# An eighth slot in the ring of loaded weight pieces, with the first tokens' mask in bf16 and two gate tiles moved to the first tokens' pool

## The chip, the cores and the metric

One Trainium2 chip, and of it one core. The metric is the device time of one execution in microseconds (us), lower is better; the time of a kernel is the median of its runs. In this text PE is TensorE, PEld its weight load, DVE is VectorE, ACT is ScalarE, POOL is GpSimd and SP is SyncE, from whose queue every DMA of this kernel is issued.

## The reference: attention with a memory, then a squared-ReLU feed-forward layer

There are 4 batches, 8 heads, 576 positions and 64 channels a head. Causal softmax attention is mixed with a linear memory read by a gate for each head; the result, 2304 tokens of 512 channels, goes through a layer of 2048 hidden units.

```python
scores = where(causal, -1e9, q @ k.T / 8)
a = exp(scores - scores.max(-1)); a /= a.sum(-1) + 1e-9
phi = lambda x: where(x > 0, x, exp(x) - 1) + 1
mem = (phi(q) @ M_prev) / (phi(q) @ z_prev + 1e-6)
g = 1 / (1 + exp(-beta))                      # for each head
x = g * mem + (1 - g) * (a @ v)               # 2304 x 512
h = x @ w_in                                  # 512 x 2048
out = maximum(h, 0) ** 2 @ w_out              # 2048 x 512
```

## The kernel before

**Weights.** They come in as 64-bit floats, seen as pairs of 32-bit words, in 32 pieces of 128 x 512 values (512 KB each): four groups of w_in pieces and four of w_out in turn, four pieces to a group. `load_weight` (L269 to 272) issues the load of a piece into the ring "raw" of `NRAW` slots, 4 KB per partition each. `to_float` (L191 to 205) makes 32-bit floats: a shift on DVE (L199) or its counterpart on ACT (L197), a rescale on ACT (L200) and a merge on DVE (L202) that writes the ring "fc" (12 slots) and is the last reader of the raw slot. After each fourth piece `weight_scale` (L221) takes products of the four pieces on PE (L228) and a root on DVE, and `halves` (L242) splits each piece into two fp16 parts, one on ACT (L246) and one on DVE (L247). `pieces` (L281) walks over the pieces; before piece n it asks for loads until `min(32, n + NRAW)` are out, so the load of piece n + NRAW - 1 is written in the program just ahead of the conversion of piece n. The first four loads are asked for inside the first tokens' load sequence `SEQ`.

**First tokens.** The first 64 positions of all batches and heads go first, in two groups (`first_tokens`, L308): scores (L339), phi (L344 to 346), the softmax with `mask0` added to the scores from PSUM (L351 to 359), the memory read with `gib` and the softmax's scale with `g1b` (L358, L371), outputs (L385 to 392), squares and a root for a scale (L397 to 403), two fp16 parts (L406, L407), and a DMA transpose into xT (L410). They have high priority. `gates` (L143) makes the gate tiles from beta.

**Then** the units of attention, one for a batch, a pair of heads and some query tiles (L453), merged with the rest of the weights and with the feed-forward layer of the first tokens, `moe(0)` (L922), whose first matmul (L973) needs both xT transposes and the first group of w_in. The blocks of 256 tokens that follow need the transposes of L724, which stand behind unit 3's results and two splits on DVE (L723).

**What sets the order.** Each engine, and SP's queue too, runs its instructions in the order in which the tile framework wrote them down; that order comes from priorities (the order of the program, the first tokens ahead) and estimated times when the kernel is compiled. Orders are also forced by hand: ACT and DVE work on pieces from 8 on, and PE's first attention work, stand behind the first tokens' operations (`gate`, `later`, `put`), and work on pieces from 16 on behind the split of piece 11.

**Memory.** `cp` holds constants for the whole kernel. The pool `rw` holds the rings raw and fc; `tp`, opened inside it, holds what the first tokens need and is closed before the pieces are converted further; the second pool of split weights, `wpl2`, is laid over its place, and the pool `late` with attention buffers of later units is laid over the place of `rw`. In both a tile waits for the former tiles under it.

```python
def pieces(n0, n1):
    for n in range(n0, n1):
        while len(loaded) < min(NU, n + NRAW):
            ahead()
        to_float(n)
```

Of the kernel before, what the change touches and what calls it, by code (L numbers as in the profile page):

```python
# [8 lines left out]
F32 = mybir.dt.float32  # L9
F32R = mybir.dt.float32r  # L10
F16 = mybir.dt.float16
BF16 = mybir.dt.bfloat16
# [6 lines left out]
B, H, S, D = 4, 8, 576, 64  # L19
# [3 lines left out]
P = 128  # L23
# [22 lines left out]
PHI = 1  # L46
ZW = D + 1
MW = 576
NRAW = 7
NFC = 12  # L50
NR0 = 16
TINY = 2.0**-80
# [17 lines left out]
GN = GB * NP  # L70
# [28 lines left out]
def fused_kernel(ctx: ExitStack, tc: tile.TileContext, t0_d, kk_d, qv_d, beta, w_in, w_out, out):  # L99
# [3 lines left out]
    cp = ctx.enter_context(tc.tile_pool(name="cp", bufs=1))  # L103
# [30 lines left out]
    def load_beta():  # L134
        nc.sync.dma_start(gpm, beta)
        gates()

    gi = cp.tile([P, H], F32, name="gi")
    gs = cp.tile([P, H], F32, name="gs")
    gib = cp.tile([P, GN], F32, name="gib")  # L140
    g1b = cp.tile([P, GN], F32, name="g1b")

    def gates():  # L143
        nc.scalar.activation(gpm, gpm, AF.Exp, scale=-1.0)
        nc.vector.tensor_scalar(out=gpm, in0=gpm, scalar1=1.0, scalar2=None, op0=ALU.add)
        for b in range(GB):
            nc.vector.tensor_copy(gib[:, b * NP : (b + 1) * NP], gp)
        nc.vector.reciprocal(gpm, gpm)
        nc.vector.reciprocal(gi, gm)
        nc.vector.tensor_scalar(out=gm, in0=gm, scalar1=-1.0, scalar2=1.0, op0=ALU.mult, op1=ALU.add)  # L150
        nc.vector.reciprocal(gm, gm)
        nc.vector.tensor_scalar(out=gs, in0=gm, scalar1=SC, scalar2=None, op0=ALU.mult)
        for b in range(GB):
            nc.vector.tensor_scalar(
                out=g1b[:, b * NP : (b + 1) * NP], in0=gp, scalar1=-1.0, scalar2=1.0, op0=ALU.mult, op1=ALU.add
            )
        nc.vector.reciprocal(g1b, g1b)

    mask0 = cp.tile([P, D], F32, name="mask0")
    nc.vector.tensor_copy(mask0[:D], mask[:D, 448 : 448 + D])  # L160
    nc.vector.tensor_copy(mask0[D:], mask[D:, 512 : 512 + D])

# [103 lines left out]
    def ring(tag, shape, dtype, bufs):  # L266
        return more[-1].tile(shape, dtype, tag=tag, name=tag, bufs=bufs)

    def load_weight(n):  # L269
        raw[n] = ring("raw", [P, 1024], U32, NRAW)  # L270
        w, r0, cs = wsrc[n]
        nc.sync.dma_start(raw[n], w[r0 : r0 + P, cs])
# [3 lines left out]
    def ahead():  # L276
        if len(loaded) < NU:
            load_weight(len(loaded))
            loaded.append(1)
# [5 lines that stand above are left out]
# [11 lines left out]
    def weights():  # L296
        with tc.tile_pool(name="rw", bufs=1, side="right") as rw:
            more.append(rw)
            with tc.tile_pool(name="tp", bufs=1, reuse_waits="tile") as tp:
                first_tokens(tp, ahead)  # L300
            yield
            yield from pieces(0, NR0)
            wpl.append(ctx.enter_context(tc.tile_pool(name="wpl2", bufs=1, reuse_waits="tile")))
            yield from pieces(NR0, NU)
        more.append(ltx.enter_context(tc.tile_pool(name="late", bufs=1, reuse_waits="tile")))
        yield

    def first_tokens(tp, ahead):  # L308
# [2 lines left out]
        ng = B // GB  # L311
        bc = [P, GN, D]
        tr, sp, et, ft, st = ({} for _ in range(5))

        for g in range(ng):
            tr[g] = tp.tile([P, TW], F32, name=f"tr{g}")
# [825 lines left out]
```

## Time and profile before

| what | value |
|---|---|
| median of 3 runs | 560.11 us (559.65 to 561.05) |
| the profiled execution | 561.7 us, of which its span is 559.9 us |
| mean granted PE clock | 0.976 of full speed |
| PE busy | 522.5 us, 93% |
| DVE busy | 451.9 us, 81% |
| ACT busy | 412.0 us, 74% |
| DMA queue of the loads | 70.57 MB, 53.7% of 16 engines' span |
| load of one weight piece | 512 KB, 6.6 us (w_in) and 7.5 us (w_out) from issue to landing, medians |

Times inside the profile count from the start of the span. A share over the whole span mixes stages: the loads and the conversion of the weights lie in the first 110 us, the rest is attention and the feed-forward layer.

### The profile page before, as it was taken

The numbers are of one execution on the slowest core, as the hardware profiler recorded it, in microseconds if no ns is written. First come the engines' busy times: TensorE is split into PE (matmuls) and PEld (weight loads), VectorE is DVE, ScalarE is ACT, GpSimd is POOL, SyncE is SP. The second block draws the span as 40 slices with busy tenths as digits, with TensorE's granted clock in tenths as the row PEclk, the third lists the DMA queues.
The fourth block names the chain that finished last, engine by engine and source line by source line (L and its number), as shares of the span: only waits on it lengthen the run. The fifth ranks groups of instructions, "written<-read, shape, count | busy, mean of one in ns | idle before, by whom it ended". The sixth has DMA issues, their size and how long they took to land.

```text
span 559.9 us, 12611 instructions
## 1 busy us (share of the span) xinstructions
PE 522.5 (93%) x4767; PEld 369.5 (66%) x4767; DVE 451.9 (81%) x1421; ACT 412.0 (74%) x884; POOL 17.8 (3%) x20
## 2 busy tenths in 40 slices
PE   5655999998999999999989999999999999999996
PEld 4544766656777767667756777667766866447766
DVE  6898879998997999999967778888686788745645
ACT  3699997894788879989867777889666734566252
POOL 1000030111010000000000000000000000000000
PEclk9967999998999999999989999999999999999999
DMA  8968931497576759988746476481755320100002
GB/s 309 405 215 247 325 109 39 124 160 186 117 157 152 174 136 158 179 171 183 131 90 150 115 138 123 76 145 47 115 94 80 91 39 1 39 1 1 1 1 75
DMA packets 133132, 71.37 MB, mean 127 GB/s; under 512 B 115408, under 2 KB 121552, under 8 KB 133072
## 3 DMA queue, kind: packets, MB, share of 16 engines
q1 hardware_dynamic: 133072, 70.57, 53.7%
q8 instruction: 37, 0.61, 0.5%
q14 instruction: 23, 0.19, 0.1%
HBM read 37.53 MB, written 4.72 MB: 75 GB/s over the span
## 4 chain that ended last, share of the span: by engine, by line
PE 53%; DVE 23%; ACT 11%; DMA 9%; issue 2%; SPq 0%; POOL 0%; DVEq 0%; ACTq 0%
PE up L973 6%; PE up L974 5%; PE up L975 5%; DVE e L604 5%; PE oacc L945 5%; PE oacc L946 5%; PE oacc L944 5%; PE acc L688 4%; DVE a L664 4%; PE seven L841 4%; ACT e L624 3%; PE sp L583 3%; DMA xT<-hl 2%; PE seven L814 2%; PE seven L813 2%; PE seven L812 2%
## 5 line engine op out<-in xcount | busy, mean ns | idle before, releaser
L973 PE MATMUL up<-xT,w 128*128 128x256 f16 x448 | 124.0, 277 | 5.7 <-DMA xT<-hl 5.1
L974 PE MATMUL up<-xT,w 128*128 128x256 f16 x448 | 123.9, 277 | 0.0
L975 PE MATMUL up<-xT,w 128*128 128x256 f16 x448 | 123.8, 276 | 0.0
L624 ACT ACTIVATE e<-e,mx 128x320 f32<-128x320 f32 (+3 forms) x128 | 77.4, 606 | 40.4 <-DVE feat L691 22.3
L944 PE MATMUL oacc<-w,gh 128*128 128x512 f16 x224 | 85.2, 380 | 0.6 <-ACT gh L982 0.5
L945 PE MATMUL oacc<-w,gh 128*128 128x512 f16 x224 | 85.3, 381 | 0.0
L946 PE MATMUL oacc<-w,gl 128*128 128x512 f16 x224 | 81.6, 380 | 0.0
L664 DVE SCALAR_TENSOR_TENSOR a<-e,a 128x128 f16<-128x128 f32 x116 | 65.8, 578 | 10.4 <-ACT a L662 9.5
L662 ACT ACTIVATE a<-e 128x128 f16<-128x128 f32 x116 | 55.0, 523 | 1.8 <-DMA aT<-a 1.4
L973 PEld LDWEIGHTS <-w 128*128 128x128 f16 x448 | 44.4, 99 | 16.3 <-DMA xT<-hl 5.6
L974 PEld LDWEIGHTS <-w 128*128 128x128 f16 x448 | 44.5, 99 | 11.5 <-issue 1.1
L975 PEld LDWEIGHTS <-w 128*128 128x128 f16 x448 | 44.5, 99 | 8.5 <-issue 0.4
L604 DVE CUSTOM_DVE_ANT_0 e<-sp,mask 128x320 f32<-128x320 f32 (+3 forms) x128 | 47.3, 422 | 2.7 <-PE sp L583 2.7
L979 ACT ACTIVATE r<-up,gam 128x512 f32<-128x512 f32 x48 | 32.4, 675 | 23.0 <-PE up L975 20.4
L688 PE MATMUL acc<-vs,aT 128*128 128x64 f16 x1138 | 43.8, 194 | 4.6 <-DMA aT<-a 3.2
L688 PEld LDWEIGHTS <-aT 128*128 128x128 f16 x1138 | 39.9, 99 | 10.1 <-DMA aT<-a 4.4
L985 DVE TENSOR_TENSOR gl<-r,gh 128x512 f16<-128x512 f32 x56 | 38.5, 688 | 5.8 <-ACT gh L982 5.3
L944 PEld LDWEIGHTS <-gh 128*128 128x128 f16 x224 | 22.0, 98 | 22.5 <-ACT gh L982 0.9
L946 PEld LDWEIGHTS <-gl 128*128 128x128 f16 x224 | 21.8, 98 | 22.3 <-DVE gl L985 0.5
L841 PEld LDWEIGHTS <-g 128*128 128x128 f16 x336 | 32.7, 98 | 5.4 <-DVE g L767 1.3
L980 ACT ACTIVATE r<-r 128x512 f32<-128x512 f32 x56 | 34.9, 624 | 0.6
L945 PEld LDWEIGHTS <-gh 128*128 128x128 f16 x224 | 22.0, 98 | 20.0 <-issue 0.3
(192 smaller groups left out, 1038.3 us busy)
## 6 DMA issues: line engine op xcount, KB each, us to landing
raw<-in_w_in_dram SPq DMA_DIRECT2D x16, 512.0 KB, 6.6
raw<-in_w_out_dram SPq DMA_DIRECT2D x16, 512.0 KB, 7.5
vv<-in_qv_dram SPq DMA_DIRECT2D x16, 320.0 KB, 3.1
kd<-in_kk_dram SPq DMA_DIRECT2D x16, 288.0 KB, 3.1
out_dram<-o SPq DMA_DIRECT2D x12, 256.0 KB, 2.1
qm<-in_qv_dram SPq DMA_DIRECT2D x8, 321.0 KB, 3.0
qm<-in_qv_dram SPq DMA_DIRECT2D x8, 193.0 KB, 4.0
vv<-in_qv_dram SPq DMA_DIRECT2D x8, 192.0 KB, 3.3
```

The source lines that it names most:

```text
L604: nc.vector.tensor_tensor_reduce(out=e[:, h, ka:kb], in0=sps[:, h, cs], in1=mask[:, 448 - q0 + ka : 448 - q0 + kb], scale=-0.125, scalar=3 ...
L624: ex = nc.scalar.activation(e[:n, h, :ke], e[:n, h, :ke], AF.Exp, bias=bs, scale=-1.0, accum_out=sm[:n, h : h + 1])
L662: nc.scalar.mul(av[:, :, o0 : o0 + w], x, SC)
L664: nc.vector.scalar_tensor_tensor(out=av[:, :, o0 + w : o0 + 2 * w], in0=x, scalar=SC, in1=av[:, :, o0 : o0 + w], op0=ALU.mult, op1=ALU.sub ...
L688: nc.tensor.matmul(acc[:n, h], lhs[:, :n], rhs, start=x == 0, stop=x == len(mms) - 1)
L841: mms.append(nc.tensor.matmul(x[:, blk], g[j][:, i0, a, blk, p], t_side(j, p, m, i1), start=j == js[0] and p == n == 0, stop=j == js[-1] a ...
L944: nc.tensor.matmul(acc[t], gh[:, u, ts], w_out_op(f, 0), start=f == f0, stop=False)
L945: nc.tensor.matmul(acc[t], gh[:, u, ts], w_out_op(f, 1), start=False, stop=False)
L946: nc.tensor.matmul(acc[t], gl[:, u, ts], w_out_op(f, 0), start=False, stop=f == f1)
L973: nc.tensor.matmul(uo, w_in_op(f, k, 0), x_op(k, 0), start=k == 0, stop=False)
L974: nc.tensor.matmul(uo, w_in_op(f, k, 0), x_op(k, 1), start=False, stop=False)
L975: nc.tensor.matmul(uo, w_in_op(f, k, 1), x_op(k, 0), start=False, stop=k == NK - 1)
```

## The change

The ring raw has eight slots in place of seven, so each load is asked for one piece sooner. The first tokens' mask is a bf16 tile in place of fp32 (128 bytes per partition less in `cp`), and `gib` and `g1b` are allocated in the first tokens' pool in place of `cp` (64 bytes per partition less there).

```diff
-NRAW = 7
+NRAW = 8
...
-    gib = cp.tile([P, GN], F32, name="gib")
-    g1b = cp.tile([P, GN], F32, name="g1b")
+    first_gates = []
 
     def gates():
+        gib, g1b = first_gates
...
-    mask0 = cp.tile([P, D], F32, name="mask0")
+    mask0 = cp.tile([P, D], BF16, name="mask0")
     nc.vector.tensor_copy(mask0[:D], mask[:D, 448 : 448 + D])
     nc.vector.tensor_copy(mask0[D:], mask[D:, 512 : 512 + D])
...
+        gib, g1b = (tp.tile([P, GN], F32, name=x) for x in ("gib", "g1b"))
+        first_gates[:] = gib, g1b
```

## Rows read from the trace of the kernel before

**Rows 1.** Busy time by stretch: us, then each engine's, PE clock, DMA share, GB/s.

```profile
0.00:60.00 60.00, 35.78 (x402) 28.38 (x403) 49.98 (x150) 44.94 (x95) 4.09 (x11) 0.83 0.86 298
60.00:110.00 50.00, 49.05 (x397) 35.51 (x395) 44.03 (x150) 44.69 (x108) 5.84 (x3) 1.00 0.44 134
110.00:160.00 50.00, 46.42 (x416) 31.98 (x413) 46.39 (x154) 38.63 (x84) 6.13 (x5) 0.97 0.74 154
```

**Rows 2.** PE's waits over the span: us in total, times, longest us.

```profile
PE up L973 <- DMA xT<-hl: 5.1, 2, 2.8
```

**Rows 3.** The chain that ended last, first 60 us: start, us, what.

```profile
2.58 7.12 DMA raw<-in_w_in_dram
...
47.12 7.17 DMA xT<-hl
54.34 0.40 PE up L973
```

**Rows 4.** Busy time by stretches of 10 us, columns as in rows 1.

```profile
10.00:20.00 10.00, 7.41 (x104) 6.34 (x104) 8.63 (x22) 5.54 (x10) 0.00 (x0) 1.00 1.04 410
...
30.00:40.00 10.00, 5.92 (x61) 4.63 (x62) 9.14 (x17) 10.00 (x19) 1.06 (x1) 0.60 0.49 144
```

**Rows 5.** SP's queue in order of time: start, us, what, count; weight loads.

```profile
9.71 2.11 SPq L272 DMA_DIRECT2D raw<-in_w_out_dram  x3
...
12.54 0.33 SPq L272 DMA_DIRECT2D raw<-in_w_out_dram  x1
...
17.23 4.16 SPq L272 DMA_DIRECT2D raw<-in_w_in_dram  x4
...
25.44 0.33 SPq L272 DMA_DIRECT2D raw<-in_w_out_dram  x1
...
36.30 0.34 SPq L272 DMA_DIRECT2D raw<-in_w_out_dram  x1
...
54.65 0.33 SPq L272 DMA_DIRECT2D raw<-in_w_out_dram  x1
...
65.25 0.33 SPq L272 DMA_DIRECT2D raw<-in_w_out_dram  x1
...
67.10 0.85 SPq L272 DMA_DIRECT2D raw<-in_w_out_dram  x2
```

**Rows 6.** SP's own waits, 0 to 36 us, then 36 to 112 us.

```profile
SPq L272 <- DMA tr<-in_t_dram: 3.9, 3, 1.8
...
SPq L272 <- DVE fc L202: 13.6, 12, 6.2
```

**Rows 7.** Timeline: conversions that wait for pieces, and updates behind; idle time in brackets.

```profile
22.77 0.77 ACT L197 ACTIVATE raw<-raw,under 128x512 uint32<-128x512 uint16 x1 [0.75 <-DMA raw<-in_w_out_dram]
...
40.03 0.43 DVE L199 TENSOR_SCALAR raw<-raw 128x512 uint32<-128x512 uint32 x1
...
59.66 0.67 DVE L199 TENSOR_SCALAR raw<-raw 128x512 uint32<-128x512 uint32 x1 [0.48 <-DMA raw<-in_w_in_dram]
...
62.73 0.48 DVE L691 SCALAR_TENSOR_TENSOR feat<-acc,sm,feat 128x64 f32<-128x64 f32 x2 [0.15 <-PE acc L688]
...
73.67 0.43 DVE L199 TENSOR_SCALAR raw<-raw 128x512 uint32<-128x512 uint32 x1 [2.97 <-DMA raw<-in_w_out_dram]
...
75.47 0.47 DVE L691 SCALAR_TENSOR_TENSOR feat<-acc,sm,feat 128x64 f32<-128x64 f32 x2 [0.34 <-PE acc L688]
```

**Rows 8.** Timeline of DVE: behind the mask's copies, the mask's reader, attention's masked scores.

```profile
5.09 0.43 DVE L345 TENSOR_SCALAR f<-f 128x512 f32<-128x512 f32 x1 [1.99 <-ACT f L344]
...
9.90 1.28 DVE L351 SCALAR_TENSOR_TENSOR w<-sp,mask 128x512 f32<-128x512 f32 x2
...
40.98 0.48 DVE L604 CUSTOM_DVE_ANT_0 e<-sp,mask 128x320 f32<-128x320 f32 x1
```

**Rows 9.** Timeline, DVE then PE: the last splits, and PE behind the next transposes.

```profile
107.66 1.41 DVE L247 SCALAR_TENSOR_TENSOR w<-fc,wout_s,w 128x512 f16<-128x512 f32 x2
...
128.90 0.28 PE L973 MATMUL up<-xT,w 128*128 128x256 f16 x1 [2.28 <-DMA xT<-hl]
```

## The prediction

> **What bounds the kernel now.** I read the busy time by stage first, then TensorE's waits, then the chain that ended last, and last the queue of SyncE (SP), which issues every load.
>
> By stage: in the first 60 us TensorE is busy 35.8 of 60 us, afterwards 49.05 of 50, then 46.42 of 50, and it stays near full [rows 1]. 60.00 - 35.78 = 24.2 us of its idle time lie in the first 60 us, 0.95 in the next 50, 3.6 in the next 50. So a change to the early loads pays only if TensorE's dense part starts sooner, or if the hole between 110 and 160 us shrinks.
>
> What it waits for: the largest named wait is for transposed tokens, xT, 5.1 us in two pieces [rows 2], 2.8 us at 54 us and 2.3 us near 129. The chain shows the start of the dense part: the second xT transpose is issued at 47.12, takes 7.17 us, and the first up-projection runs at 54.34 [rows 3]. That transpose ends a long sequence on ScalarE (ACT) and VectorE (DVE), which are busy 10.00 and 9.14 us of the ten from 30 to 40 us [rows 4]. The weight pieces and the first tokens share those two engines: until then a free slot is not what is short.
>
> **The eighth slot, by the load it moves.** There are 32 pieces of 512 KB, piece n and its load being "n". Loads 0 to 6 find empty slots; now 7 does as well.
>
> *Loads 4 to 13.* They don't wait for slots. Load 4 goes at 9.71, the moment when load 1 has landed (2.58 + 7.12 = 9.70); load 8 goes at 17.23, though its slot (piece 1, converted at 11.14 in 0.69 us) was free at 11.83 [rows 3, 5]. In the first 36 us the load instruction waited 3.9 us for the first tokens' transfers [rows 6], and from 10 to 20 us the transfers run at 410 GB/s [rows 4]. Another slot gives them neither bandwidth nor an earlier turn, so I take 0. Bounds: load 7 may pass the kd load just before it and go right behind load 6, at 9.71 + 2.11 = 11.82 in place of 12.54; that is 0.72 of the 0.75 us for which ACT waits on it at 22.77 [rows 5, 7]. DVE, which is busy until it takes that piece, covers it. Loads 7 and 8 may pass unit 1's qm and vv, which are then one 1.27 us step later (four loads from 17.23, the last 3.83 later: 3.83 / 3); that unit's exp comes at 42.49, more than 20 us after. Also 0.
>
> *Loads 14 to 31.* From 25.44 on each stands right behind the conversion that frees its slot: 12 waits, 13.6 us together [rows 6]. Load 15 goes at 36.30 because piece 8 is converted at 35.59 to 36.28. With eight slots load n waits for piece n-8, so it takes about the turn that n-1 has now: 15 goes at 25.44 in place of 36.30 if it stands ahead of the first transpose in SP's queue, 16 at 36.30, 24 at 54.65, 30 at 65.25, 31 at 67.10 [rows 5]. The number of pieces between 36 and 45 us stays eight, so the second transpose meets the same traffic; between 25 and 31 there is one piece more, while SP merely stands at the first transpose.
>
> What waits for a piece from 14 on? Three places, all on DVE: 0.14 us at 40.03 (the instruction before ended at 38.60 + 1.29 = 39.89), 0.48 at 59.66 and 2.97 at 73.67 [rows 7]; ACT has no such wait after 22.77. Sum 3.59 us. Load 30 landed at about 73.6; 1.85 us sooner it leaves 1.1 of the 2.97, so some 2.5 us can vanish.
>
> What is late next? Behind the 0.48 stands the update at 62.73, which waits for TensorE anyway. Behind the 2.97 stand three root operations of 0.15 us, one subtraction of 0.67 whose input ACT finishes at 73.23 + 0.64 = 73.87, and then the update at 75.47, which even now waits 0.34 us for TensorE's value product [rows 7]. With today's order on DVE this update starts at 75.47 whether or not the piece was early. So both stalls are covered by TensorE, and of 3.59 us only the 0.14 at 40.03 reaches the second transpose. Lower bound nothing, upper bound the whole hole of 3.6 us that TensorE has between 110 and 160 us. I take 0.1: the row after each stall names TensorE.
>
> The Trainium skill says otherwise at first sight: Perfetto Trace Analysis, Optimization Strategy, reads the same gap repeating on an engine that should be saturated as a possible lack of buffers. Twelve gaps before one load instruction look like that; were they all on the path the sum would be 13.6 us, against 0.1 by the rows. By that rule the gaps would have to be on an engine that should be full, and here they are in SP's queue.
>
> **The mask in bf16.** Two copies of 0.18 us at 2.7 to 3.1, followed by 1.99 us in which DVE waits for ACT [rows 8]: whatever they cost now is hidden; without that cover 0.2 us at most. Its reader takes 1.28 us for two instructions of 512 elements, 1.25 ns an element; the score instruction, which already adds a bf16 mask to fp32 from PSUM, starts its next after 0.41 us for 320 elements, 1.28 ns [rows 8]. The two differ by 0.03 x 1024 = 0.03 us. I take 0, between -0.6 (half the time) and +0.03.
>
> **Places.** The two gate tiles issue the same instructions as before. The first tokens' pool, 64 bytes per partition larger, is later overlaid by the second pool of split weights, first written at 74.58; the first tokens' last operation precedes the transpose at 47.12, a margin of 27 us. The pool of slots grows by 4 KB and is overlaid by the late attention buffers, first written at 125.93, behind the last read of a piece at 109.07 (107.66 + 1.41) [rows 9]. 0, unless the margins vanish.
>
> **Sum.** The profiled execution took 561.7 us (span 559.9, 1.8 around it); it lies 0.3% over the median of 560.11. 561.7 - 0.1 - 0 - 0 = 561.6, on the median's scale 560.0. The order of instructions on each engine is made at compile time from estimated times, so it may move by a few places; small gains are easier found than losses where DVE loses a stall, and I put the time at 559.7.
>
> **Rivals.**
> *A, forecast: everything is covered.* 558.5 to 561.7, chance 0.43. "No change" means within 0.3%, 1.7 us, which is about what a measurement of this kernel can tell.
>
> *B, faster: the order changes so that DVE's stalls are filled.* With the piece there sooner, conversions that now run at 79.89 may be placed in the gap at 70.7 to 73.67, and the last weights be split before unit 3's values arrive. Then the pair of splits at 107.66 (1.41 us) leaves the DVE chain that ends in the transposes behind which TensorE stands until 128.90 [rows 9]. It is worth 1.41 (558.7) up to that hole of 3.6 (556.5); I put it at 557.6. For it: DVE is full from 112 to 126 us and TensorE starved behind it. Against: ACT, too, is full around the stall. Chance 0.38. The rule of Perfetto Trace Analysis in the Trainium skill points this way; its price here is the one worked out from the rows.
>
> *C, slower: a load blocks SP's queue.* SP takes its DMAs in order. The load that waits for piece 16 goes at 54.65 [rows 5] and now stands behind the second transpose (47.12). Should the load with that wait, now 24, be placed ahead of it, the transpose goes 54.65 + 0.33 - 47.12 = 7.9 us later: 568. It decides as soon as that one load precedes the transpose. Against: its place in the program is the same step 16. Chance 0.06.
>
> *D, slower by less: piece 15 ahead of the first tokens.* With 15 landed by about 31 us, its shift (0.43 [rows 7]), its rescale (0.66) and its conversion (0.69) may be placed ahead of the second group's squares on ACT (41.15) and its root on DVE: at most 1.78 us, 561.9; with its traffic in front of the transpose, one step of 1.27 more, 563.2. Pieces from 16 on can't, as they are held behind piece 11's split. Chance 0.13, all counted as slower.
>
> **Numbers.** Faster 0.38 (B), same 0.43 (A), slower 0.19 (C and D). Likeliest A, 559.7, its own range 558.5 to 561.7. From B's lower end down to its far tail and from D upward about 0.1 each is left out: 556.2 to 562.4.
>
> **What would show it.** Right: load 15 near 25 us, loads from 16 on one turn earlier; the stall at 73.67 gone or under 1.2 us; the second transpose still near 47 and the up-projection near 54; TensorE's hole near 125 still some 3 us. B: that hole under 2 us and the last split before 107. C: the second transpose at 55. D: it at 48 to 50. The prediction is wrong if the up-projection's start moves by over 1.7 us, or if TensorE's idle time after 60 us does, above all through an order of instructions that these rows don't foretell.

## The result: slower by 1.2%

| | before | after |
|---|---|---|
| median | 559.88 us (4 runs, 559.60 to 561.05) | 567.48 us (4 runs, 567.15 to 568.39) |
| ratio, 95% interval | | 1.0118 (1.0094 to 1.0143) |
| the profiled execution, its span | 561.7 us, 559.9 us | 567.19 us, 565.4 us |

The spans differ by 5.5 us and the medians by 7.6, since the profiled execution of before lay 1.8 us above its median and that of after 0.3 below. The ratio is an estimate of its own and not the quotient of the two medians, which is 1.0136; its interval holds both. In the changed kernel line numbers from L311 on are higher by two: L690 is L688 of before, L693 is L691, L975 is L973.

Where the time goes is seen first in the busy time by stretch of the changed kernel (columns as in rows 1):

```profile
0.00:60.00 60.00, 35.26 (x411) 28.46 (x412) 50.53 (x151) 44.75 (x95) 5.49 (x11) 0.83 0.89 307
60.00:110.00 50.00, 45.32 (x342) 32.83 (x340) 37.30 (x132) 41.64 (x102) 1.79 (x3) 0.97 0.32 101
110.00:160.00 50.00, 46.19 (x412) 30.57 (x411) 44.68 (x152) 37.68 (x78) 4.63 (x4) 1.00 0.74 156
```

TensorE's busy time in the first and the third stretch is within 0.6 us of [rows 1]. In the second, TensorE is busy for 45.32 of 50 us, where it had 49.05, with 342 matmuls recorded instead of 397. It is a stretch in which it had almost no idle time to lose.

The loads themselves went, but for one, as a ring with one slot more should make them. SP's queue of the changed kernel:

```profile
9.76 2.59 SPq L272 DMA_DIRECT2D raw<-in_w_out_dram  x4
12.58 0.33 SPq L272 DMA_DIRECT2D raw<-in_w_in_dram  x1
...
22.67 2.83 SPq L272 DMA_DIRECT2D raw<-in_w_out_dram  x4
31.95 1.35 SPq L412 DMA_TRANSPOSE xT<-hl  x1
36.70 3.67 SPq L272 DMA_DIRECT2D raw<-in_w_in_dram  x4
...
48.00 1.24 SPq L412 DMA_TRANSPOSE xT<-hl  x1
...
62.06 0.33 SPq L444 DMA_DIRECT2D vv<-in_qv_dram  x1
62.48 0.38 SPq L272 DMA_DIRECT2D raw<-in_w_out_dram  x1
...
64.45 2.26 SPq L272 DMA_DIRECT2D raw<-in_w_out_dram  x3
```

Load 7 stands with 4 to 6, load 15 is the fourth of the group at 22.67, loads 29 to 31 go at 64.45, and both transposes stand where they should, the second ahead of the loads from 24 on. The one is load 28, at 62.48: it stands behind a load for attention (vv). What changed most is what VectorE does with piece 30. Its timeline in the changed kernel:

```profile
65.67 2.49 DVE L202 SCALAR_TENSOR_TENSOR fc<-raw 128x512 uint32<-128x512 uint32 x4
71.86 0.43 DVE L199 TENSOR_SCALAR raw<-raw 128x512 uint32<-128x512 uint32 x1 [3.71 <-DMA raw<-in_w_out_dram]
72.21 0.69 DVE L202 SCALAR_TENSOR_TENSOR fc<-raw 128x512 uint32<-128x512 uint32 x1
72.81 0.28 DVE L231 TENSOR_REDUCE win_e<-gr 128x1 f32<-128x128 f32 x1
...
73.42 0.29 DVE L210 TENSOR_REDUCE win_e<-gr 128x1 f32<-128x128 f32 x1
...
80.15 0.47 DVE L693 SCALAR_TENSOR_TENSOR feat<-acc,sm,feat 128x64 f32<-128x64 f32 x2 [5.28 <-PE acc L690]
```

and the same engine, before:

```profile
69.61 0.29 DVE L231 TENSOR_REDUCE win_e<-gr 128x1 f32<-128x128 f32 x1 [0.71 <-PE gr L228]
69.82 0.68 DVE L202 SCALAR_TENSOR_TENSOR fc<-raw 128x512 uint32<-128x512 uint32 x1
70.42 0.28 DVE L210 TENSOR_REDUCE win_e<-gr 128x1 f32<-128x128 f32 x1
```

Before, the first step of group 4's root (L231) came first and the shift of piece 30 (L199) after it; its wait of 2.97 us at 73.67 [rows 7] held up nobody but VectorE (run 2 below bears this out). Now the shift stands in front of both steps of the root. Its load landed 1.8 us earlier (71.86 against 73.67), as foretold, but VectorE came to it 2.55 us earlier (71.86 - 3.71 = 68.15 against 73.67 - 2.97 = 70.70), so that it waits longer than before, and for the root TensorE waits too. TensorE's timeline after:

```profile
73.15 0.23 PE L209 MATMUL gr<-identb,win_e 128*128 128x128 bf16 x1 [3.57 <-DVE win_e L231]
73.76 0.27 PE L975 MATMUL up<-xT,w 128*128 128x256 f16 x1 [0.38 <-DVE win_e L210]
...
74.54 0.42 PE L977 MATMUL up<-xT,w 128*128 128x256 f16 x1
74.75 0.42 PE L975 MATMUL up<-xT,w 128*128 128x256 f16 x1
...
78.14 1.97 PE L690 MATMUL acc<-vv,aF 64*128 64x64 f32 x12
```

and before, at the same matmul:

```profile
70.75 0.27 PE L973 MATMUL up<-xT,w 128*128 128x256 f16 x1 [0.57 <-DVE win_e L210]
```

This up-projection starts at 73.76 instead of 70.75, 3.01 us late. The update behind it (L693) starts at 80.15 instead of 75.47, 4.68 late, so another 1.67 are lost in between. There the matmuls come 0.21 us apart (74.54, 74.75), and the profile has the granted clock for it. Changed kernel, stretch by stretch:

```profile
68.00:73.00 5.00, 1.08 (x16) 0.90 (x15) 1.29 (x4) 5.00 (x15) 0.00 (x0) 1.00 0.79 286
...
74.00:77.30 3.30, 3.30 (x18) 2.36 (x16) 0.84 (x3) 3.30 (x7) 0.00 (x0) 0.51 0.00 0
```

After a stretch in which TensorE was busy 1.08 of 5 us, its clock is at 0.51 for 3.3 us, the lower of its two levels (1.2 GHz). At full clock that work would have taken 3.3 x 0.51 = 1.7 us; 1.6 are lost. By 80 us the changed kernel is thus 3.01 + 1.67 = 4.68 us behind, of 5.5 at the end, and the chain that ended last goes through these ten microseconds (start, us, what):

```profile
65.44 6.33 DMA raw<-in_w_out_dram
71.86 0.43 DVE raw L199
72.29 0.60 DVE fc L202
73.15 0.24 PE gr L209
...
78.21 1.90 PE acc L690 x12
```

This is a reading so far: 970 of VectorE's 1261 instructions, 516 of ScalarE's 735 and 3319 of TensorE's 4517 stand in another place of their engine's order than before, and the loss could be spread among them. The lag isn't steady either: at the next transposes, those of L724, it is 127.14 - 124.22 = 2.92 us. A kernel with nearly the same order is needed for the comparison; run 4 is one.

### The profile page after: what moved, and what is told of

It reads as the page before. It is cut to its first block, busy times and chain, and to the rows that moved or that the text cites. A ratio compares the mean times of both kernels' runs of the same rounds, so it can differ in the third digit from the quotient of the medians.

```text
span 565.4 us, 12618 instructions
## 1 busy us (share of the span) xinstructions
PE 520.8 (92%) x4767; PEld 367.2 (65%) x4767; DVE 449.6 (80%) x1421; ACT 411.8 (73%) x884; POOL 14.8 (3%) x20
## 4 chain that ended last, share of the span: by engine, by line
PE 37%; DVE 29%; ACT 17%; DMA 12%; issue 3%; SPq 1%; POOL 0%; ACTq 0%; DVEq 0%
DVE e L606 5%; DVE a L666 4%; DMA aT<-a 4%; PE oacc L948 4%; ACT e L626 4%; PE oacc L947 4%; PE up L975 4%; PE oacc L946 4%; PE up L976 4%; PE up L977 4%; PE acc L690 3%; DMA vv<-in_qv_dram 3%; PE seven L843 3%; DMA raw<-in_w_out_dram 3%; DVE gl L987 3%
## 5 line engine op out<-in xcount | busy, mean ns | idle before, releaser
L975 PE MATMUL up<-xT,w 128*128 128x256 f16 x448 | 123.7, 276 | 5.6 <-DMA xT<-hl 5.2
L977 PE MATMUL up<-xT,w 128*128 128x256 f16 x448 | 123.6, 276 | 0.0
L975 PEld LDWEIGHTS <-w 128*128 128x128 f16 x448 | 44.4, 99 | 16.1 <-DMA xT<-hl 3.7
L977 PEld LDWEIGHTS <-w 128*128 128x128 f16 x448 | 44.4, 99 | 6.5
L690 PE MATMUL acc<-vs,aT 128*128 128x64 f16 x1138 | 42.3, 193 | 5.9 <-DMA aT<-a 3.9
L690 PEld LDWEIGHTS <-aT 128*128 128x128 f16 x1138 | 39.1, 98 | 11.2 <-DMA aT<-a 4.5
L693 DVE SCALAR_TENSOR_TENSOR feat<-acc,sm,feat 128x64 f32<-128x64 f32 x128 | 29.1, 276 | 10.0 <-PE acc L690 9.9
L946 PEld LDWEIGHTS <-gh 128*128 128x128 f16 x224 | 21.9, 98 | 21.2 <-ACT gh L984 1.6
```

Source lines behind the costliest of these rows:

```text
L690: nc.tensor.matmul(acc[:n, h], lhs[:, :n], rhs, start=x == 0, stop=x == len(mms) - 1)
L946: nc.tensor.matmul(acc[t], gh[:, u, ts], w_out_op(f, 0), start=f == f0, stop=False)
L975: nc.tensor.matmul(uo, w_in_op(f, k, 0), x_op(k, 0), start=k == 0, stop=False)
L977: nc.tensor.matmul(uo, w_in_op(f, k, 1), x_op(k, 0), start=False, stop=k == NK - 1)
```

## The experiments

Three theories. **1**: the loss comes from the new order of instructions, and from one place in it (1a) or from more (1b); the slot, its traffic and the places in memory cost nothing. **2**: the slot's earlier transfers or their places in SP's queue cost it. **3**: the bf16 mask or the moved tiles do. Each ratio is to the kernel before, run on the same chip; its medians there were 561.02 us for runs 1 to 4, 561.31 for 5 to 8 and 560.27 for 9 and 10.

| run | median us | ratio, 95% interval |
|---|---|---|
| 1 mask and gate tiles alone | 561.25 | 1.0011 (0.9987 to 1.0035) |
| 2 eight slots, old order | 559.85 | 0.9990 (0.9966 to 1.0013) |
| 3 seven slots, new order | 576.79 | 1.0282 (1.0259 to 1.0305) |
| 4 eight slots, shift held back | 562.17 | 1.0020 (1.0003 to 1.0037) |
| 5 before, shift moved ahead | 567.90 | 1.0118 (1.0090 to 1.0147) |
| 6 run 2, shift moved ahead | 562.74 | 1.0023 (1.0002 to 1.0045) |
| 7 new order, load 30 earlier | 563.28 | 1.0042 (1.0025 to 1.0059) |
| 8 as 7, order written anew | 563.04 | 1.0042 (1.0016 to 1.0067) |
| 9 new order, filled wait | 569.22 | 1.0157 (1.0121 to 1.0193) |
| 10 the changed kernel again | 567.05 | 1.0110 (1.0086 to 1.0134) |

**1. The mask and the gate tiles alone.** The change without its first line:

```diff
 NRAW = 7
-    mask0 = cp.tile([P, D], F32, name="mask0")
+    mask0 = cp.tile([P, D], BF16, name="mask0")
+        gib, g1b = (tp.tile([P, GN], F32, name=x) for x in ("gib", "g1b"))
```

> Seven slots as before, with the bf16 mask and the moved gate tiles alone; every engine's order is that of before. Theory 1 (the loss comes from the new order of instructions on VectorE and TensorE, the slot and the places cost nothing): 559.5 to 561, no change. Theory 2 (the eighth slot's own transfers cost the time): also 559.5 to 561. Theory 3 (the places of the mask and the gates cost it, by conversions or by a buffer that comes free later): 564 to 568.

561.25 us, no change beyond the interval (0.9987 to 1.0035). Theory 3 falls.

**2 and 3. Slot and order apart.** The order of the four compute engines is written out: every instruction gets an edge behind the one before it on its engine, which places it and adds no wait on another engine. Run 2 gives the changed kernel the order of before, run 3 gives the kernel before the order of the changed one. SP's queue isn't written out; there only the weight loads differ.

```diff
     fused_kernel(tc, *args)
+    in_order(tc)
```

> The whole change, eight slots and all, but TensorE, VectorE, ScalarE and GpSimd issue their instructions in the order that they had before; only the weight loads stand earlier in SP's queue, as in the changed kernel. Theory 1 (order): the loss goes, 557 to 561; TensorE between 60 and 110 us is busy for about 49 us of 50 again (45.3 in the changed kernel). Below 559 would say that the shorter stalls at 40, 60 and 73 us are worth something once the order is kept. Theory 2 (the eighth slot's transfers or their places in SP's queue): 566 to 568, as in the changed kernel. Theory 3 (places in memory): 564 to 568.

> Seven slots and the old places, but the four compute engines issue their instructions in the order of the changed kernel. Theory 1 (order): 566 to 571, the loss is there without the slot; the shift of piece 30 on VectorE waits for its load, which one slot fewer starts later, so that the wait there is at least the 3.71 us of the changed kernel. Theory 2 and theory 3: 559.5 to 561.

Run 2: 559.85 us; the whole change is there and the loss is gone. VectorE's timeline and TensorE's stretch in run 2:

```profile
68.61 0.29 DVE L231 TENSOR_REDUCE win_e<-gr 128x1 f32<-128x128 f32 x1
...
69.61 0.42 DVE L199 TENSOR_SCALAR raw<-raw 128x512 uint32<-128x512 uint32 x1
...
74.47 0.48 DVE L691 SCALAR_TENSOR_TENSOR feat<-acc,sm,feat 128x64 f32<-128x64 f32 x2 [0.22 <-PE acc L688]
```

```profile
60.00:110.00 50.00, 48.87 (x393) 34.92 (x393) 44.37 (x151) 45.50 (x109) 5.78 (x4) 1.00 0.42 129
```

The shift of piece 30 no longer waits. The update starts 1.0 us earlier than in [rows 7], but so does the root ahead of the shift (68.61 for 69.61), and the end doesn't move by anything that can be measured. So the wait that the slot takes away was worth nothing, and the slot's own transfers cost nothing that shows. SP's queue still differs in one place from that of the changed kernel: in run 2 load 28 goes at 58.00, ahead of the load for attention. Run 4 below has the changed kernel's queue (load 28 at 62.21, loads 29 to 31 from 64.74) and hardly any loss, so with these two theory 2 falls. Run 3 has a loss without the slot, and a larger one than expected, 15.8 us; it doesn't say what the order costs with eight slots. The order that was written for eight slots meets loads that come a turn later:

```profile
64.47 0.43 DVE L199 TENSOR_SCALAR raw<-raw 128x512 uint32<-128x512 uint32 x1 [4.07 <-DMA raw<-in_w_in_dram]
...
81.33 0.43 DVE L199 TENSOR_SCALAR raw<-raw 128x512 uint32<-128x512 uint32 x1 [5.47 <-DMA raw<-in_w_out_dram]
```

**4. The one place.** One edge more in the changed kernel:

```diff
+            x = put(n, "v", nc.vector.tensor_scalar(out=u0, in0=u0, scalar1=29, ...))
+            if n == 30:
+                tc.add_manual_dep(x.ins, gate["root4"].ins.name, AFTER, ...)
...
+            root4 = nc.vector.reciprocal(win_s[:, j], x)
+            if g == 4:
+                gate["root4"] = root4
```

> The changed kernel with one edge more: VectorE's shift of piece 30 comes behind the last step of the scale of group 4 (its reciprocal), as before; nine places of VectorE's order change and none on another engine. Theory 1a (the whole loss is TensorE's wait for that scale): 559.5 to 562.5. Theory 1b (that wait is 3.6 to 4.7 us of it, and the rest arises in the order of later parts): 562.5 to 564.5. Theory 2 and theory 3: 566 to 568.5, with the wait gone from its place and TensorE waiting as long a little later.

562.17 us, 1.0020: 0.98% of the 1.18% is gone with nine places of VectorE's order, and thousands of others are as in the changed kernel. The two engines in run 4 (lines are two to four higher than before: L233 is L231, L977 is L973, L695 is L691, L728 is L724), and its clock in the stretch where it had been 0.51:

```profile
69.29 0.29 DVE L233 TENSOR_REDUCE win_e<-gr 128x1 f32<-128x128 f32 x1 [0.24 <-PE gr L230]
...
71.19 0.43 DVE L199 TENSOR_SCALAR raw<-raw 128x512 uint32<-128x512 uint32 x1 [0.42 <-DMA raw<-in_w_out_dram]
...
74.96 0.48 DVE L695 SCALAR_TENSOR_TENSOR feat<-acc,sm,feat 128x64 f32<-128x64 f32 x2 [0.45 <-PE acc L692]
```

```profile
70.25 0.27 PE L977 MATMUL up<-xT,w 128*128 128x256 f16 x1 [0.38 <-DVE win_e L212]
```

```profile
74.00:77.30 3.30, 3.30 (x20) 2.10 (x21) 2.85 (x12) 3.30 (x7) 0.00 (x0) 1.00 0.00 0
```

The root comes first again, the up-projection starts at 70.25, the clock stays at 1.00 and the update is back at 74.96. The transposes of L724, first in the changed kernel (there L726), then in run 4:

```profile
127.14 2.85 SPq L726 DMA_TRANSPOSE xT<-hl  x2
```

```profile
121.58 2.84 SPq L728 DMA_TRANSPOSE xT<-hl  x2
```

The changed kernel is 80.15 - 74.96 = 5.19 us behind run 4 at the update, 127.14 - 121.58 = 5.56 at these transposes and 565.4 - 559.5 = 5.9 at the end of the span. Nearly the whole difference arises in one place and stays. That is 1a, apart from 0.2%.

**5 and 6. The same place, made on purpose.** In the order of before, the shift of piece 30 is moved three places ahead, in front of the root; run 5 has seven slots, run 6 eight. VectorE's order there, by lines:

```diff
-L202  L669  L673  L231  L202  L210  L199 (piece 30)  L216
+L202  L669  L673  L199 (piece 30)  L231  L202  L210  L216
```

> The kernel before, seven slots, with VectorE's shift of piece 30 moved three places ahead, in front of the first step of group 4's root; nothing else moves on any engine. Theory 1 (a shift that waits for its load in front of a root for which TensorE stands is the loss): the load lands near 73.6 us, the shift stands there, TensorE stands from about 69.2 to 74.5, at least 4 us, and starts again at half its clock: 565 to 569. Rival (the wait is covered there too, and the loss sits in the thousands of other places that moved): 559.5 to 562.

> Eight slots, the order of before on the four compute engines, and the same three-place move of piece 30's shift. Its load goes out at 64.3 there and has landed by 69.6 us. Theory 1 (the wait, not the place, costs): the shift waits for less than 1.5 us and 559.5 to 562.5. Rival (the place in the order costs by itself): 563 or more.

Run 5: 567.90 us and 1.0118, the same ratio as that of the change, from one instruction moved. VectorE and TensorE in run 5:

```profile
72.62 0.43 DVE L199 TENSOR_SCALAR raw<-raw 128x512 uint32<-128x512 uint32 x1 [4.21 <-DMA raw<-in_w_out_dram]
```

```profile
73.30 0.29 PE L209 MATMUL gr<-identb,win_e 128*128 128x128 bf16 x1 [4.51 <-DVE win_e L231]
74.10 0.37 PE L973 MATMUL up<-xT,w 128*128 128x256 f16 x1 [0.51 <-DVE win_e L210]
```

Run 6: 562.74 us, a little above its expectation of 559.5 to 562.5. With the load there a turn earlier the same place costs little, since the wait is under 1 us:

```profile
69.81 0.43 DVE L199 TENSOR_SCALAR raw<-raw 128x512 uint32<-128x512 uint32 x1 [0.97 <-DMA raw<-in_w_out_dram]
```

So it isn't the place alone. It is the place with a transfer that is still under way. The changed kernel, with the same eight slots, waits 3.71 us there: VectorE comes to the shift at 68.15 and not at 68.84 (69.81 - 0.97), and load 30, issued at the same time in both (65.44, and 65.43 in run 6), lands 2.05 us later. It goes there among loads 29 to 31 back to back, where run 6 issues them at 63.35, 65.43 and 67.28. That this makes it slower isn't shown.

**7 and 8. The same order, the load earlier.** Piece 30 is loaded ahead of 28 and 29. Run 7 keeps every compute engine in the changed kernel's order, run 8 lets it be written anew.

```diff
-            load_weight(len(loaded))
+            load_weight((*range(28), 30, 28, 29, 31)[len(loaded)])
```

> The changed kernel with every compute engine in the changed kernel's order, but piece 30 is loaded ahead of pieces 28 and 29. Its load then stands with the four issued near 54 us and lands before 68. Theory 1 (the wait for this one load is the whole loss): the wait of 3.71 us at 71.86 is gone, TensorE stands for under 1.5 us near 69.5, and 560 to 563.5. Rival (the changed order costs by itself, wherever the load lands): 566 to 568.5.

> As the run before it, but the order of the compute engines is left to be written anew with that load order; five places of VectorE and nine of ScalarE change, none of TensorE. The shift of piece 30 then stands four places earlier still. Theory 1: 560 to 563.5 if its load lands by about 66 us, and 563 to 567 if it lands later, with VectorE's wait for it ahead of group 4's merges. Rival: 566 to 568.5.

563.28 and 563.04 us, within what theory 1 allows: of 1.18% some 0.76% go, with the order untouched in run 7. In run 7 its load goes at 62.84, the place that load 28 had, and lands 3.5 us later; it isn't among the four near 54 us, as had been expected, which are pieces 24 to 27. Its shift finds it landed:

```profile
62.84 0.38 SPq L272 DMA_DIRECT2D raw<-in_w_out_dram  x1
```

```profile
68.54 0.42 DVE L199 TENSOR_SCALAR raw<-raw 128x512 uint32<-128x512 uint32 x1
...
69.47 0.28 DVE L231 TENSOR_REDUCE win_e<-gr 128x1 f32<-128x128 f32 x1
```

**9 and 10. Is the clock a part of the price?** TensorE gets matmuls to do while it waits; their result is overwritten unread.

```diff
+        for _ in range(48 if g == 4 else 0):
+            nc.tensor.matmul(gr[:, 1], identb, identb, start=True, stop=True)
         nc.vector.reduce_max(out=x, in_=gr[:, 0], axis=AX.X)
```

> The changed kernel in its own order, with 48 matmuls of 128 x 128 more on TensorE, whose result is overwritten unread; they stand just ahead of the matmul that waits for group 4's root, so that TensorE works through most of that wait. The wait for piece 30 stays on VectorE. Theory 1 with a second part (after the wait of 3.57 us the granted clock is 0.51 from 74.0 to 77.3 us, and the matmuls there come 0.21 us apart in place of 0.11, which costs 1.6 us more): the clock stays at 1.00 there and the time falls by 1.6 us of the changed kernel's, to 565.5 to 566.5 if that one runs at 567.5. Rival (the slow matmuls are covered, as VectorE is late anyway; the wait is the whole loss): within 0.5 us of the changed kernel.

> The changed kernel once more, beside the run with filled matmuls on the same chip: 566 to 569.5, 1.009 to 1.014 of the kernel before, its clock about 0.5 from 74.0 to 77.3 us.

Run 10 repeats the loss. Run 9 missed: 569.22 us, not faster than run 10 but slower. Its runs spread from 566.94 to 573.52, and the profiled one is the highest of them. TensorE in it (L232 is the filling), and its clock afterwards:

```profile
69.89 2.84 PE L232 MATMUL gr<-identb 128*128 128x128 bf16 x48
75.23 0.23 PE L209 MATMUL gr<-identb,win_e 128*128 128x128 bf16 x1 [2.51 <-DVE sm L671]
```

```profile
77.30:80.00 2.70, 2.70 (x15) 1.89 (x14) 0.00 (x0) 2.70 (x6) 0.13 (x1) 0.53 0.00 0
```

VectorE's wait was 4.45 us in that execution, the filling covered 2.84 us and left a gap of 2.51, and the clock fell behind it all the same. So the run doesn't take the clock's fall away and can't say what the fall costs. Why it is slower than run 10 isn't shown; the wait for piece 30 is 4.45 us in its profiled execution and 2.49 in that of run 10. That the slow matmuls make 1.6 us of the loss rests on their spacing and on the update that waits for them (5.28 us at 80.15), not on an experiment.

## Why the prediction was wrong

- **The time**: 559.7 was foretold, 556.2 to 562.4; 567.48 was measured, which only "slower", at 0.19, allows for, and neither of the two mechanisms behind that 0.19 took place. C: the second transpose is issued at 48.00, not 55. D: 48.00 is at the edge of the 48 to 50 that it named, but the up-projection of the dense part starts at 53.89, 0.45 earlier than before, so nothing was lost there. The hole between 110 and 160 us stayed, 3.8 us for 3.6. What came was the prediction's own last sign of being wrong: TensorE's idle time between 60 and 110 us went from 0.95 to 4.68 us, through an order of instructions that its rows don't foretell.
- **Loads 4 to 31**: right but for one. Load 7 went with 4 to 6, load 15 at 22.67 to 25.50, the last three a turn earlier, and load 30 landed 1.8 us sooner (1.85 foretold). Load 28 didn't take load 27's turn: it went at 62.48, where it goes at 58.00 in run 2.
- **Mask and places**: 0 agrees with run 1, within its interval.
- **The covered stalls**: right as a statement on the old order. In run 2 the wait of 2.97 us is gone and the time is 0.9990 of before (0.9966 to 1.0013). That agrees with the rows, and not with the 13.6 us that the prediction put on these gaps for the case that all of them were on the path. By the rule of the Trainium skill that was weighed there (Perfetto Trace Analysis, Optimization Strategy), a gap that repeats on the engine which should be full can mean too few buffers. Run 2, which has one buffer more, doesn't bear the rule out for these gaps, and they are in SP's queue, which needn't be full.
- **The step that failed** is "What is late next?", with its sentence "With today's order on DVE this update starts at 75.47 whether or not the piece was early", and the sum that took this order over: it "may move by a few places; small gains are easier found than losses where DVE loses a stall". The shift of piece 30 moved by a few places, ahead of both steps of the root, and three places are enough (run 5). The prediction looked at what stands behind the wait of piece 30 and found it harmless. It didn't look at what stands just ahead of it, one and three instructions away: L210 and L231, the steps of group 4's root, for which TensorE waits, with no slack. Had it asked what a wait of some 3 us costs in front of them, the trace had the answer: TensorE already stood there for 0.57 us (at 70.75, before), so that nearly all of it would be its own. Run 5 measures such a wait, 4.21 us of VectorE there, at 6.6 us (567.90 - 561.31), and run 4 takes 5.5 us back (1.18 - 0.20 = 0.98% of 561.02).
- **Rival B**, at 0.38, went by a new order too, but by one that fills VectorE's stalls; here the new order made the stall longer, 3.71 us for 2.97, and put it in front of a producer. The place seems to follow the load: in run 8, where load 30 is earlier still and the order is written anew, the shift stands in front of all five merges (67.36, the merges from 67.71), where the changed kernel has it behind four of them. In the changed kernel the piece landed 3.71 us after VectorE had come to its place (2.49 in run 10). Why the order was written so, by which estimated times, no trace shows.
- **What stays open**: 0.2 to 0.4% with the root or the load mended (runs 4 and 7), against none in the old order (run 2). It may lie in the rest of the new order; no run separates it. What the clock's fall costs by itself is open too. No run was faster than the kernel before beyond its interval.

## What to carry to other kernels

Where the order of instructions is written at compile time, a change of buffers can also be a change of order, as here. Ask of each instruction that waits for a transfer not only who stands behind it today but which producers of the critical engine stand within a few places of it, and price the wait in front of them. If the price is high, one edge that holds the waiting instruction behind that producer is cheap insurance (run 4: 5.5 us with one edge). And before a slower result is put down to the change, run the new resources in the old order: run 2 told the slot from the order.

## What the runs showed of the hardware

In these runs a long wait of TensorE was followed by slow matmuls. After gaps of 2.5 to 6.2 us (2.51 in run 9, 2.89 in run 10, 3.57 in the changed kernel, 4.51 in run 5, 2.99 and 6.23 in run 3) the matmuls behind them ran for some 3 us or more at a granted clock near 0.5, the lower of its two levels (1.2 GHz), in some from the first one on, in others from up to 1.4 us later; run 5 has it from 73 us on:

```profile
73.00:74.00 1.00, 0.29 (x1) 0.13 (x2) 1.00 (x4) 0.90 (x2) 0.00 (x0) 0.50 0.02 8
74.00:77.30 3.30, 3.20 (x16) 2.21 (x16) 1.11 (x5) 2.64 (x5) 0.00 (x0) 0.50 0.00 0
```

After gaps of 0.4 to 1.1 us at the same matmuls (before, and runs 1, 2, 4, 6, 7 and 8) it was 1.00 there. For gaps in between, the length of the last one doesn't tell: at the first up-projection behind the transposes of L724, the changed kernel waits 1.79 us (131.62) and runs on at 1.00 from 132 to 136 us, while run 6 waits 1.76 us (128.88) and runs at 0.50 from 130 to 134.
